# Batch 0 of an attention and mixing kernel: one group of scores weighted by a product on VectorE, fewer zero matmuls, one key tile for two query tiles

## The chip, the cores and the metric

The kernel runs on one core of a Trainium2 chip. The metric is the device time of one execution in microseconds (us); less is better. The core has five engines that the text names as the profile does: PE (TensorE, matmuls and transposes; PEld is its weight load), DVE (VectorE), ACT (ScalarE), POOL (GpSimd) and SP (SyncE, which here only starts transfers). Each engine works through its own instructions in order, and waits on semaphores for the others. Matmuls write to PSUM, from where VectorE or ScalarE fetch the result.

## The reference

The inputs are q, k, v of shape (4 batches, 8 heads, 768 tokens, 64) and the weights of a mixing layer; the output is (4, 768, 512) in float32. Cut to what matters:

```
rel  = pos[:, None] - pos[None, :]                  # 768 x 768
keep = (pos[None, :] < 8) | ((rel >= 0) & (rel < 96))
dist = where(global and not local, 96, |rel|)
scores = q @ k.T / 8 - slopes[h] * dist ; masked to -1e9 where not keep
a   = softmax(scores) ; x = (a @ v), heads side by side      # (B, 768, 512)
theta = x @ w_theta
y   = w_tok_r @ (x * cos(theta)) + w_tok_i @ (x * sin(theta))
u   = x + y
out = u + max(u @ w_ch, 0)
```

A query sees the 95 tokens before it, itself, and the first 8 tokens. With tiles of 128 tokens, a query tile therefore needs two key tiles: its own, and the one before it, whose first 8 rows can give way to the 8 global tokens.

## The kernel before, in words

**Tiles and groups.** There are six token tiles (NT). Heads are taken in pairs, `h0` = 0, 2, 4, 6. Scores stand with the keys on the partitions. `GROUPS` (line 198) lists the blocks (query tile, 1 for the key tile before it or 0 for its own) of a head pair in three groups: group 0 has (0,0), (1,1), (1,0), groups 1 and 2 have four blocks each. A group of both heads fills one PSUM tile `ps_w` (`ps_wide`, two buffers), which ScalarE turns to exponentials.

**The distance term, in two ways.** In batches 1 to 3, `att_scores` writes the scores alone, ScalarE takes the exponential into `e`, and `att_mul` multiplies it on VectorE by `wmask`, the exponential of minus slope times distance (also zero where masked), giving `p`. In batch 0, `att_bias` (line 242) first writes the distances into PSUM by matmuls of a scaled identity (`ident_d`) with `dist`, the scores are added on top, and ScalarE's exponential (line 272) gives `p` at once, with no product. `make_wmask` (line 192) makes the weights of one head by one ScalarE instruction.

**Steps of a head pair.** `att_transpose` (line 208) turns q and k of the pair on PE into two `ps_tr` PSUM buffers (of two) and copies them out, kT on ScalarE and qT on VectorE in batch 0. `att_extras` (line 231) makes the keys "before, with global rows" out of kT, on POOL (for pair 0 on VectorE); the groups 1 and 2 read them. `prepare_v` does the same for v. `att_values` (line 294) multiplies the probabilities with v into `ps_mm` buffers, `att_norm` (line 327) divides by the sums on VectorE, giving `x_sb`. `turn_x` (line 338) transposes a block of x on PE (into `ps_tr`) and copies it to `xT`; the variant "both" splits the copy between VectorE and ScalarE.

**Mixing.** `mix_theta` (line 356) multiplies xT with w_theta into `ps_w`, in pieces by dc (0 to 3, the head pair), and ends with cosine and sine on ScalarE (lines 372 and 373); `mix_z` multiplies them with x on VectorE; `setup_wtok` transposes the token weights, `mix_tok` sums over tokens, `mix_ch` does the last layer. In batches 1 to 3 attention of the next batch is laid between the mixing of the one before (`attend_beside`).

**What sets the order.** `K` keeps the order of the program text on each engine, so the order is written out by hand. Batch 0 stands at lines 500 to 545: in a loop over `h0` = 2, 4, 6 come the scores of groups 0 and 1, the values and normalisation of the pair before, the transposes of the next pair, the scores of group 2 and `turn_x`. Loads go through POOL's queue (`load_heads`, `load_wtok`, `load_weight`), in the order of the text, between POOL's copies.

**Zero matmuls.** `keep_warm(n)` issues n matmuls of zeros into a `ps_mm` buffer, `keep_warm_tr(n)` into a `ps_tr` buffer. Eight stand at the start of the program and two ahead of the first scores (line 509).

Of the kernel before, what the change touches and what calls it, by code (L numbers as in the profile page):

```python
# [16 lines left out]
def kernel(  # L17
# [13 lines left out]
    nc = tc.nc  # L31
    B, H, S, D = q.shape
    T = 128
# [20 lines left out]
    K = tc.keep_in_program_order  # L54
# [200 lines left out]
    def att_scores(b, h0, g_):  # L255
        qT, kT = qTs[b, h0], kTs[b, h0]
        blocks = GROUPS[g_]
        n = len(blocks)
        bias = b == 0
        if bias and (h0, g_) not in biased:  # L260
            att_bias(h0, g_)
        ps = biased[h0, g_] if bias else ps_wide()
        for i_, (it, prev) in enumerate(blocks):
            kc = it * T if prev == 0 else (0 if it == 1 else S + (it - 2) * T)
            for hh in range(2):
                R = slice(D * hh, D * (hh + 1))
                K(nc.tensor.matmul(ps[:, hh, i_ * T:(i_ + 1) * T],  # L267
                                   lhsT=kT[R, kc:kc + T], rhs=qT[R, it * T:(it + 1) * T],
                                   start=not bias, stop=not bias or i_ == n - 1))
        if bias:  # L270
            p = abuf.tile([T, 2, 4 * T], BF, name="p", bufs=6)
            K(nc.scalar.activation(p[:, :, 0:n * T], ps[:, :, 0:n * T], AF.Exp, scale=scale))  # L272
            probs[b, h0, g_] = p
            return
        e = abuf.tile([T, 2, 4 * T], BF, name="e", bufs=3)
        K(nc.scalar.activation(e[:, :, 0:n * T], ps[:, :, 0:n * T], AF.Exp, scale=scale))  # L276
        exps[b, h0, g_] = e
        att_mul(b, h0, g_)
# [58 lines left out]
    def turn_x(b, dc, by_dma, eng=nc.vector.tensor_copy):  # L337
# [10 lines left out]
        if eng == "both":  # L348
            K(nc.vector.tensor_copy(out=xT[:, 0:2 * T], in_=pt[:, 0:2 * T]))  # L349
            K(nc.scalar.copy(out=xT[:, 2 * T:], in_=pt[:, 2 * T:]))  # L350
        else:
            K(eng(out=xT, in_=pt))
# [147 lines left out]
    for h in range(6):  # L500
        make_wmask(h)
# [3 lines left out]
    att_transpose(0, 0, extras=False, between=lambda: att_bias(0, 1), cuts=(43, T))  # L505
# [3 lines left out]
    keep_warm_tr(2)  # L509
# [7 lines left out]
    for h0 in (2, 4, 6):  # L517
        att_scores(0, h0, 0)
        att_scores(0, h0, 1)
# [3 lines left out]
        if h0 < 6:  # L523
# [5 lines left out]
            att_scores(0, h0, 2)  # L529
# [3 lines left out]
    att_scores(0, 6, 2)  # L533
    mix_theta(0, 0, 0, 2)
    turn_x(0, 2, False, nc.scalar.copy)
    for h in range(6, H):
        make_wmask(h)
# [5 lines left out]
    mix_theta(0, 2, 0, 3)  # L543
    mix_theta(0, 0, 2, 3)
    turn_x(0, 3, False, "both")
# [89 lines left out]
```

## Time and profile before

| | |
|---|---|
| median of 3 runs | 175.93 us (175.57 to 175.95) |
| profiled execution | 177.43 us |
| its span, first to last instruction | 175.7 us |
| busy: PE, DVE, ACT, POOL | 165.6, 111.7, 103.8, 60.6 us |
| batch 0, first values of pairs 0, 2, 4, 6 on PE at | 13.20, 17.67, 22.20, 24.95 us |
| first cosine of batch 0 on ACT at | 28.88 us |

The profile is of one execution; times in it are us from the first instruction. A row of the timeline is: start, duration, engine, line of the kernel, operation, tile written and tiles read, shape and count; where rows of one kind follow each other they are merged, and the duration is that of all. Matmuls are pipelined: the row of a matmul is longer than the time until the next one starts, so the distance from start to start is what one takes of PE. A row of the waits is: who waited, for whom, us in total, how many times, the longest. In the slices each digit is a fortieth of the span, in tenths busy. The list of DMA issues gives for each transfer the time from issue to landing.

### The profile page before, as it was taken

The page shows a single profiled execution, that of the slowest core. Times are in us where ns is not written, and L with a number is a line of the kernel's source. Part 1 is how long each engine was busy: PE and PEld are TensorE (multiplying, and loading weights), DVE is VectorE, ACT ScalarE, POOL GpSimd, SP SyncE. Part 2 cuts the span into 40 slices and gives each one's busy share as a digit, 9 for nine tenths or more (in the row PEclk, how much of TensorE's full clock was granted, in tenths as well). Part 3 has the DMA queues.
Part 4 walks back from the last instruction along what each step waited for, and adds up shares of the span by engine and source line. Part 5 has one row for each costly group of instructions (what it writes and reads, how often), then busy time and mean ns, then how long its engine had stood idle before and what let it go on. Part 6 is the DMA issues. An engine that isn't in the chain of part 4 may idle for free.

```text
span 175.7 us, 4158 instructions
## 1 busy us (share of the span) xinstructions
PE 165.6 (94%) x1740; PEld 88.1 (50%) x1740; DVE 111.7 (64%) x205; ACT 103.8 (59%) x121; POOL 60.6 (35%) x99
## 2 busy tenths in 40 slices
PE   7889999899999999999998979999999999999992
PEld 2346665566465554445454544546555544444441
DVE  7756654975768784857567691857568784734353
ACT  5697889947777553797846712797756807500010
POOL 8986695004571400049716100049118000000000
PEclk9999999999999999999999999999999999999999
DMA  5999999999999944117999996116999433312325
GB/s 150 185 174 191 212 207 209 191 189 177 131 142 161 193 84 149 63 60 92 174 98 180 153 147 208 63 60 90 174 93 160 104 97 118 119 30 60 90 109 189
DMA packets 57058, 24.05 MB, mean 137 GB/s; under 512 B 43088, under 2 KB 54096, under 8 KB 57040
## 3 DMA queue, kind: packets, MB, share of 16 engines
q0 software_dynamic: 35328, 12.45, 65.8%
q1 hardware_dynamic: 21440, 10.95, 32.0%
q10 hardware_dynamic: 272, 0.39, 0.6%
q8 instruction: 13, 0.21, 0.5%
q14 instruction: 5, 0.04, 0.1%
HBM read 25.69 MB, written 6.29 MB: 182 GB/s over the span
## 4 chain that ended last, share of the span: by engine, by line
PE 56%; DMA 20%; ACT 9%; DVE 7%; POOL 4%; issue 2%; ACTq 0%
PE ps_mm L399 21%; PE ps_mm L441 10%; PE ps_w L364 9%; DMA v_sb<-in_v_dram 7%; DMA uTd<-u 6%; PE ps_tr L215 4%; PE ps_w L267 4%; DMA k_sb<-in_k_dram 4%; PE ps_w L315 3%; ACT kT L225 3%; DMA first<-in_q_dram 3%; ACT cs L373 2%; DVE w_tokT L117 2%; PE ps_w L252 2%; PE ps_mm L315 2%
## 5 line engine op out<-in xcount | busy, mean ns | idle before, releaser
L399 PE MATMUL ps_mm<-zri,w_tokT 128*128 128x512 bf16 x288 | 69.8, 380 | 0.1
L276 ACT ACTIVATE e<-ps_w 128x1024 bf16<-128x1024 f32 (+1 forms) x36 | 33.0, 951 | 19.6 <-PE ps_w L267 19.6
L399 PEld LDWEIGHTS <-w_tokT 128*128 128x128 bf16 x288 | 25.7, 98 | 28.2 <-issue 0.6
L233 POOL COPY kT<-kT 128x512 bf16<-128x512 bf16 x15 | 9.3, 622 | 64.6 <-ACT kT L225 64.6
L372 ACT ACTIVATE cs<-ps_w,halfpi 128x1024 bf16<-128x1024 f32 x12 | 13.4, 1115 | 19.7 <-PE ps_w L364 19.6
L441 PE MATMUL ps_mm<-w_ch_bf,uTd 128*128 128x512 bf16 x88 | 22.6, 380 | 1.4 <-DMA uTd<-u 1.4
L364 PE MATMUL ps_w<-w_theta_bf,xT 128*128 128x512 bf16 x96 | 22.9, 380 | 0.6 <-DVE xT L349 0.4
L404 DVE TENSOR_TENSOR u<-x_sb,ps_mm 128x512 bf16<-128x512 bf16 x24 | 16.2, 681 | 10.5 <-PE ps_mm L399 10.5
L288 DVE TENSOR_TENSOR p<-e,wmask 128x1024 bf16<-128x1024 bf16 x24 | 17.4, 725 | 8.5 <-ACT e L276 8.4
L380 DVE TENSOR_TENSOR zri<-cs,x_sb 128x1024 bf16<-128x1024 bf16 x24 | 16.1, 687 | 9.1 <-ACT cs L372 7.7
L444 DVE SCALAR_TENSOR_TENSOR o_sb<-ps_mm,u 128x512 f32<-128x512 f32 (+1 forms) x25 | 16.6, 664 | 2.8 <-PE ps_mm L441 2.7
L267 PEld LDWEIGHTS <-kT 64*128 64x128 bf16 x352 | 10.0, 94 | 14.7 <-issue 11.0
L267 PE MATMUL ps_w<-qT,kT 64*128 64x128 bf16 x352 | 16.2, 218 | 0.5 <-DVE kT L234 0.5
L225 ACT COPY kT<-ps_tr 128x768 bf16<-128x768 bf16 (+2 forms) x17 | 12.9, 765 | 4.9 <-PE ps_tr L215 4.9
L315 PEld LDWEIGHTS <-p 128*128 128x128 bf16 x352 | 12.9, 97 | 4.5 <-issue 0.8
L364 PEld LDWEIGHTS <-xT 128*128 128x128 bf16 x96 | 8.9, 98 | 11.3 <-DVE xT L349 0.6
L441 PEld LDWEIGHTS <-uTd 128*128 128x128 bf16 x88 | 8.0, 98 | 10.4 <-DMA uTd<-u 1.5
L80 POOL DMA_DIRECT2D v_sb<-in_v_dram x10 | 13.0, 1305 | 0.0
L286 DVE TENSOR_TENSOR p<-e,wmask 128x768 bf16<-128x768 bf16 x12 | 6.7, 559 | 9.9 <-ACT e L276 9.9
L272 ACT ACTIVATE p<-ps_w 128x1024 bf16<-128x1024 f32 (+1 forms) x12 | 11.3, 953 | 1.7 <-PE ps_w L267 1.2
L373 ACT ACTIVATE cs<-ps_w 128x1024 bf16<-128x1024 f32 x12 | 12.2, 1020 | 0.0
L91 POOL COPY v_pv<-v_sb 128x520 bf16<-128x520 bf16 x15 | 9.3, 620 | 8.3 <-DMA v_sb<-in_v_dram 8.3
(80 smaller groups left out, 192.4 us busy)
## 6 DMA issues: line engine op xcount, KB each, us to landing
out_dram<-o_sb SPq DMA_DIRECT2D x23, 256.0 KB, 2.2
q_sb<-in_q_dram POOLq DMA_DIRECT2D x6, 384.0 KB, 8.5
k_sb<-in_k_dram POOLq DMA_DIRECT2D x6, 384.0 KB, 10.1
v_sb<-in_v_dram POOLq DMA_DIRECT2D x6, 384.0 KB, 13.8
w_nat<-in_moe_w_tok_r_dram POOLq DMA_DIRECT2D x1, 1152.0 KB, 12.2
w_nat<-in_moe_w_tok_i_dram POOLq DMA_DIRECT2D x1, 1152.0 KB, 13.4
v_sb<-in_v_dram POOLq DMA_DIRECT2D x4, 192.0 KB, 7.3
q_sb<-in_q_dram POOLq DMA_DIRECT2D x3, 192.0 KB, 6.8
```

The costliest lines, as they stand in the source:

```text
L225: K(op(out=dst.rearrange("a (p t) -> a p t", t=NT)[:, p0:p1, :], in_=src.rearrange("a (t p) -> a p t", t=NT)[:, p0:p1, :]))
L267: K(nc.tensor.matmul(ps[:, hh, i_ * T:(i_ + 1) * T], lhsT=kT[R, kc:kc + T], rhs=qT[R, it * T:(it + 1) * T], start=not bias, stop=not bias ...
L276: K(nc.scalar.activation(e[:, :, 0:n * T], ps[:, :, 0:n * T], AF.Exp, scale=scale))
L288: K(nc.vector.tensor_mul(p.rearrange("a h (r x) -> a h r x", r=2), e.rearrange("a h (r x) -> a h r x", r=2), wmask[:, hs, None, T:3 * T].t ...
L315: K(nc.tensor.matmul(dst, lhsT=lhsT, rhs=rhs, start=(i_ == 0), stop=(i_ == len(mms) - 1)))
L364: K(nc.tensor.matmul(pth[:, s2, :], lhsT=xTs[b][:, dc, c:c + T], rhs=w_theta_bf[:, dc, :], start=(dc == 0), stop=(dc == NC - 1)))
L373: K(nc.scalar.activation(cs[:, :, 1, :], pth, AF.Sin))
L380: K(nc.vector.tensor_mul(zris[b][:, st:st + 2, wi, :].rearrange("a s (c d) -> a s c d", d=T), cs[:, :, wi, :].rearrange("a s (c d) -> a s ...
L399: K(nc.tensor.matmul(acc, lhsT=w_tokT[wi][:, st, tt * T:(tt + 1) * T], rhs=zris[b][:, st, wi, :], start=(done[b, tt] == 0), stop=(done[b, ...
L404: K(nc.vector.tensor_add(us[b][:, tt, :].rearrange("a (c d) -> a c d", d=T), x_sb[b][:, :, tt, :], acc.rearrange("a (c d) -> a c d", d=T)))
L441: K(nc.tensor.matmul(pc[:, 0:N], lhsT=uT[:, c:c + T], rhs=w_ch_bf[:, dc, cols], start=(dc == 0), stop=(dc == NC - 1)))
L444: K(nc.vector.scalar_tensor_tensor(o_sb, in0=pc[:, 0:N], scalar=0.0, in1=us[b][:, tt, cols], op0=ALU.max, op1=ALU.add))
```

## The change

In batch 0, group 1 of every head pair is made as in the later batches: no distance matmuls, the exponential into `e`, and a product with `wmask` on VectorE. In the loop this product stands after the normalisation of the pair before and the transposes of the next. All eight heads' `wmask` are made at the start. Ahead of the first scores, the bias matmuls of group 1 between the transposes of q and k give way to one zero matmul, and the two zero matmuls before the scores to one in a `ps_mm` buffer, which needs no `ps_tr` buffer. In all batches, the first key tile is used for the query tiles 0 and 1 in one matmul of 256 columns. `turn_x` of the last block copies both parts on VectorE, and the theta matmuls of dc 2 for the second pair of tiles stand after its transposes instead of before.

```diff
-    def att_scores(b, h0, g_):
+    def att_scores(b, h0, g_, mul=True):
         qT, kT = qTs[b, h0], kTs[b, h0]
         blocks = GROUPS[g_]
         n = len(blocks)
-        bias = b == 0
+        bias = b == 0 and g_ != 1
         if bias and (h0, g_) not in biased:
             att_bias(h0, g_)
         ps = biased[h0, g_] if bias else ps_wide()
-        for i_, (it, prev) in enumerate(blocks):
+
+        runs = [(0, 2)] + [(2, 1)] if g_ == 0 else [(i_, 1) for i_ in range(n)]
+        for i_, w in runs:
+            it, prev = blocks[i_]
             kc = it * T if prev == 0 else (0 if it == 1 else S + (it - 2) * T)
             for hh in range(2):
                 R = slice(D * hh, D * (hh + 1))
-                K(nc.tensor.matmul(ps[:, hh, i_ * T:(i_ + 1) * T],
-                                   lhsT=kT[R, kc:kc + T], rhs=qT[R, it * T:(it + 1) * T],
+                K(nc.tensor.matmul(ps[:, hh, i_ * T:(i_ + w) * T],
+                                   lhsT=kT[R, kc:kc + T], rhs=qT[R, it * T:(it + w) * T],
                                    start=not bias, stop=not bias or i_ == n - 1))
...
         exps[b, h0, g_] = e
-        att_mul(b, h0, g_)
+        if mul:
+            att_mul(b, h0, g_)
...
-        if eng == "both":
+        if eng == "halves":
             K(nc.vector.tensor_copy(out=xT[:, 0:2 * T], in_=pt[:, 0:2 * T]))
-            K(nc.scalar.copy(out=xT[:, 2 * T:], in_=pt[:, 2 * T:]))
+            K(nc.vector.tensor_copy(out=xT[:, 2 * T:], in_=pt[:, 2 * T:]))
...
-    for h in range(6):
+    for h in range(H):
         make_wmask(h)
...
-    att_transpose(0, 0, extras=False, between=lambda: att_bias(0, 1), cuts=(43, T))
+    att_transpose(0, 0, extras=False, between=lambda: keep_warm(1), cuts=(43, T))
     make_ident_d(2, 6)
     att_extras(0, 0, nc.vector)
     prepare_v(0, 0, nc.vector)
-    keep_warm_tr(2)
+    keep_warm(1)
     att_scores(0, 0, 0)
     att_scores(0, 0, 1)
...
     for h0 in (2, 4, 6):
         att_scores(0, h0, 0)
-        att_scores(0, h0, 1)
+        att_scores(0, h0, 1, mul=False)
         att_values(0, h0 - 2, apart=True)
         att_norm(0, h0 - 2)
         att_norm(0, h0 - 1)
...
                 load_heads(1, 0, 4)
-            att_scores(0, h0, 2)
+        att_mul(0, h0, 1)
+        att_scores(0, h0, 2)
+        if h0 < 6:
             turn_x(0, h0 // 2 - 1, False)
     load_heads(1, 4, 4)
     load_weight(w_ch_bf, moe_w_ch)
-    att_scores(0, 6, 2)
     mix_theta(0, 0, 0, 2)
     turn_x(0, 2, False, nc.scalar.copy)
-    for h in range(6, H):
-        make_wmask(h)
 
     K(nc.scalar.activation(halfpi_e, halfpi, AF.Sin))
     att_values(0, 6, apart=True)
     att_norm(0, 6)
     att_norm(0, 7)
-    mix_theta(0, 2, 0, 3)
+    mix_theta(0, 2, 0, 2)
     mix_theta(0, 0, 2, 3)
-    turn_x(0, 3, False, "both")
+    turn_x(0, 3, False, "halves")
+    mix_theta(0, 2, 2, 3)
     mix_theta(0, 0, 3, 4)
     mix_theta(0, 2, 3, 4)
```

## The prediction

> I write 4.1 for group 1 of the head pair that begins with head 4, and "exp 4.1" for its exponential on ScalarE. Times are us from the start of the span; times of the changed kernel are estimates, worked out from the rows named. An instruction that hands over on its own engine frees it some 0.05 before its recorded end, and a hand-over between engines takes about 0.05: both are read off neighbouring rows.
>
> **What bounds the kernel now.** First the page's busy shares and its slices (one digit is 4.39 us):
>
> ```profile
> span 175.7 us, 4158 instructions
> ...
> PE 165.6 (94%) x1740; PEld 88.1 (50%) x1740; DVE 111.7 (64%) x205; ACT 103.8 (59%) x121; POOL 60.6 (35%) x99
> ...
> PE   7889999899999999999998979999999999999992
> ...
> DMA  5999999999999944117999996116999433312325
> ```
>
> TensorE holds the kernel: no other engine is above 64%, and PE's only low digits lie in the first slices, once past the middle, and at the end. Whatever PE saves in batch 0 is therefore worth its time, if no one else becomes late. Second, PE's waits in the first 46 us, all of them:
>
> ```profile
> PE ps_mm L137 <- DVE zero L123: 1.2, 1, 1.2
> PE ps_w L267 <- DVE kT L234: 0.5, 1, 0.5
> PE ps_tr L215 <- DVE q_sb L503: 0.4, 1, 0.4
> PE ps_w L252 <- ACT p L272: 0.4, 1, 0.4
> PE ps_w L364 <- DVE xT L349: 0.4, 1, 0.4
> PE ps_tr L114 <- DVE w_tokT L117: 0.3, 1, 0.3
> PE ps_w L364 <- ACT cs L373: 0.2, 1, 0.2
> ```
>
> 3.4 us of 46, half of it before the first transposes; between 12.4 and 28 the list has none. Third, the timeline of PE in one turn of the batch-0 loop (pair 4):
>
> ```profile
> 15.77 0.49 PE L347 MATMUL ps_tr<-ident,x_sb 128*128 128x128 bf16 x6
> 16.11 0.49 PE L252 MATMUL ps_w<-dist,ident_d 128*128 128x384 bf16 x2
> 16.53 0.34 PE L267 MATMUL ps_w<-qT,kT 64*128 64x128 bf16 x6
> 16.82 0.59 PE L252 MATMUL ps_w<-dist,ident_d 128*128 128x512 bf16 x2
> 17.34 0.40 PE L267 MATMUL ps_w<-qT,kT 64*128 64x128 bf16 x8
> 17.67 0.27 PE L315 MATMUL ps_mm<-v_sb,p 128*128 128x65 bf16 x3
> ```
>
> From start to start: turn_x 0.34, bias of group 0 0.42, its scores 0.29, bias of group 1 0.52, its scores 0.33. One turn lasts 4.47 (values start at 13.20, 17.67, 22.20). The bias of group 1 is what the change takes out.
>
> **The parts that cost or give nothing by themselves.** *One key tile for two query tiles*: per group 0, six matmuls of 128 columns become two of 256 and two of 128. Rows of 6, 8 and 16 scores last 0.34, 0.40 and 0.62: 0.055 per pair of heads, and a 512-column matmul follows another after 0.216 (L364, four in 0.86), so 128 columns cost 0.054. The pair's time is the columns', and they stay. I take 0. The bound above is the whole 0.055 of the one pair dropped in each of the 12 groups after batch 0: 0.66 gained; nothing is added that could lose. *Eight weights first*: eight wmask rows 0.414 apart from 3.62 end at 7.04 instead of 6.2; ScalarE next works at 7.69, so the 1.49 idle before it hides them. Without that cover they cost 0.83. Two rows, 0.94, leave ScalarE at 25.84. *Scores 6.2 ahead of the last loads*: they stand in other queues than those loads (POOL's), so nothing.
>
> **The opening.** k's transposes started at 7.12, 0.53 after q's ended (6.59), behind two 512-column bias matmuls; one zero matmul is 0.216 plus about 0.1 for the change of shape, so they start near 6.90, and ScalarE's first kT piece 7.47 instead of 7.69. The other zero matmul, 0.3 with its change of shape, lies in the wait for that piece, from 7.2; the first scores follow the piece's end (7.85): 7.89 instead of 8.32, where two zeros stood in the way. Exp 0.0 follows the second kT piece, 8.28 (was 8.70). VectorE's kT extras still stand behind six ident_d rows (end 8.48), so scores 0.1 start 8.98 (was 9.17) and exp 0.1 ends 10.44 (was 10.63). Now the first new wait: VectorE's product for 0.1 (0.69, row L288) comes at 10.50 ahead of the copy qT of pair 2, which moves from 10.51 to 11.12 and ends at 12.06 instead of 11.45. Behind it wait scores 2.0, which start at 12.11 instead of 11.59. But bias 2.1, which sat until 12.30 waiting for exp 0.2 and then took 0.53, is gone: scores 2.1 follow at 12.28 (were 12.87), and the values of pair 0 start at 12.61 instead of 13.20. Exp 2.1 is even (13.25 against 13.30), bound by exp 2.0.
>
> **The loop.** I carry the same durations on. VectorE: the two normalisations take 1.40 up to qT (13.74 to 15.14), and follow the values: qT of pair 4 from 14.56 to 15.51. ScalarE: kT of pair 4 from 14.34 (end of the transposes; exp 2.1 ends 14.27), exp 2.2 15.16 to 16.18. PE: turn_x at 15.19 (was 15.77), bias and scores 4.0 until 16.23. Scores 4.1 need the PSUM buffer of exp 2.2 (16.23) and POOL's kT extras, which take 0.61 and 0.21 after kT (in the trace 15.78 to 16.67), so 15.20 to 16.08. Here is the second new wait. The product 2.1 stands in VectorE's queue behind qT, at 15.46, at the very time of POOL's copies. The trace shows what that costs, in two views of one place:
>
> ```profile
> 92.62 0.69 DVE L288 TENSOR_TENSOR p<-e,wmask 128x1024 bf16<-128x1024 bf16 x1 [0.35 <-ACT e L276]
> 93.53 1.10 DVE L288 TENSOR_TENSOR p<-e,wmask 128x1024 bf16<-128x1024 bf16 x1 [0.22 <-ACT e L276]
> ```
>
> ```profile
> 94.16 0.95 POOL L92 COPY v_pv<-v_sb 8x520 bf16<-8x520 bf16 x1
> 96.56 0.61 POOL L92 COPY v_pv<-v_sb 8x520 bf16<-8x520 bf16 x1
> ```
>
> A product beside POOL's copies takes 1.10 instead of 0.69, and a POOL copy 0.95 instead of 0.61: 0.41 and 0.34. The page GPSIMD Engine Reference of the Trainium skill (section "Key points") speaks against the change in the same sense: POOL shares its SBUF interfaces with VectorE and contends with instructions of two SBUF inputs. It gives no price, so by the rule alone there would be a loss of unknown size, down to none.
>
> I take the rows' price: POOL is done at 16.42, scores 4.1 start at 16.47 (16.23 without contention), values of pair 2 at 16.80 (were 17.67), with the product done at 16.56. What waits behind the product, the copy xT, ends at 17.06 before the transposes at 17.58 want its buffer. The next turn by the same steps: kT of pair 6 from 18.53, exp 4.2 19.35 to 20.37, POOL done at 20.62, scores 6.1 at 20.67, values of pair 4 at 21.00 (were 22.20). The turn falls from 4.47 to 4.20: PE gives 0.64 back, but 0.37 goes to waits for kT, exp and POOL.
>
> **The end of the loop.** Scores 6.2 end 22.61, exp 6.2 22.67 to 23.69 (was to 24.93); the product 6.1 stands behind the normalisations (22.97 to 23.66), beside POOL's DMA issues, where products kept 0.69 in the trace (80.98, during an issue of 80.31 to 81.76). The values of pair 6 start at 23.75 (were 24.95). xT of dc 2 ends on ScalarE at 24.77, the table load, 1.28, at 26.05: earlier than needed, since the two wmask rows no longer precede it. Six theta matmuls (1.29) then stand ahead of the last turn_x; it needs the normalisation, 25.76, and starts at 25.81; the two moved theta matmuls (0.43) fill the time of its copies, which removes PE's 0.4 wait for xT. The second half of xT on VectorE is 512 columns between the rows 0.29 (256) and 0.56 (768): 0.42, ends 27.0. The theta matmuls for dc 3 start at 26.68 (were 28.23), the first cs at 27.32 (was 28.88): 1.56 earlier.
>
> **What comes after.** From there ScalarE's cs rows (six in 6.0), VectorE's copies and PE's mixing follow each other as before. They need transfers that do not move: the weights of load_wtok(0), issued 13.45, land 12.2 later, 25.65, wanted at 27.6; those of load_wtok(1), 17.85 and 13.4, land 31.25, wanted at 32.4 (were 34.0); keys of batch 1, 23.10 and 12.2, land 35.3, wanted at 36.9. POOL issues them no later than now. w_theta, 10.09 and 10.0, lands 20.1, wanted at 22.5. None is late, so the 1.56 stays; I round to 1.6. Sum against the profiled execution: 177.43, of which 175.7 is span and 1.73 lies around it, gives 175.8. That execution is 1.5 above the median of the three, 175.93; a shift of the same size there gives 174.3.
>
> Bounds of the loop's costs: without the contention the two scores x.1 come 0.24 and 0.25 earlier, gain 2.05; with the contention also on the product beside DMA issues (as the ident_d rows at 3.5, 0.68 to 0.75 against 0.18) values of pair 6 slip 0.55, gain 1.0. So 173.9 to 174.9, and 173.3 with the 0.66 of the merged matmuls.
>
> **Rivals.** *Turn_x waits for qT's buffer.* It shares its PSUM slots with kT's and qT's transposes. Now it starts as kT's copy ends (15.72, start 15.77), before qT's does (16.09): it gets kT's slot. The zeros that also took one of these slots are gone, and the order in which slots come free may turn. Then turn_x starts 0.37 later in two turns: gain 0.9, 175.0. *A transfer takes the gain back.* Half the gain or all of it, if load_wtok(1) or the keys land 1.1 to 1.5 later than now or a transposing transfer of u (PE waits 1.4 for one at 105) meets other loads: 175.0 to 176.0, I write 175.6. For it: the DMA digits are 9 until 62. Against: POOL's queue only gets earlier.
> *Slower: TensorE's clock falls back.* The page's granted clock reads full throughout, but the zeros lie 0.43 apart until 4.6 (eight rows in 3.60) and 0.216 later; twelve transposes of q take 0.80 and those of k 0.53. So the array was at half speed until about 6.5, five us after its first work. The change takes 0.53 (bias) + 0.43 (two zeros) - 2 x 0.216 (the new ones), 0.53 us, of work from 6.6 to 9.0 and leaves a pause of 0.8 before scores 0.1, where the longest now is 0.5. If the array then runs at half speed for as long again, 5.3 us from 9.3, it loses 2.65, of which the 0.7 wait for qT absorbs a part: 1.9 more, 176.3. It decides from 4.6 us of half speed on. Against it, the pause is short beside the time it took to warm. The page "TensorE: Matmul & The Clock Gate" ("What's actually happening") asks for an idle window of about 3.4 us before half rate returns; by that rule this rival is out, and no row here tests it.
>
> **How the numbers follow.** The forecast of 174.3 (own range 173.8 to 174.9) gets 0.57; turn_x 0.14; a transfer 0.10, half of it within 0.2% (0.35 us, about what a measurement of this kernel can tell from no change); the clock 0.16; 0.03 for a loss that I don't see. Faster 0.57 + 0.14 + 0.05 = 0.76, same 0.05, slower 0.19. The range runs from the merged matmuls' bound, 173.3, to 176.0: it leaves out the clock, most of the 0.03 and little below.
>
> **What would show it.** Right: values of pairs 0, 2, 4, 6 near 12.6, 16.8, 21.0, 23.75; products of 1.1 in the turns of pairs 2 and 4; first cs near 27.3; later stages shifted whole. Wrong: turn_x starting after the end of qT; transposes of pair 2 at twice their 0.8 (clock); PE waiting for w_nat or k_sb after 28; scores of six columns' tiles not 0.34 but much shorter.

## The result, and the profile after

The changed kernel takes 174.37 us (median of 11 runs), the kernel before 176.18 us in the same series (11 runs). The ratio is 0.9877, with a 95% interval of 0.9848 to 0.9907: 2.2 us less, between 1.6 and 2.7. The forecast was 174.3 us, 1.6 us less than 175.93. The predicted time is met closely in part by luck: the kernel before came out 0.25 us higher in this series, and the gain is larger than the sum of the prediction's steps. (Ratios leave out executions that lie more than 1.5% above the fastest of the same kernel.)

The profiled execution took 173.99 us, 172.2 of it span. Its page, with the same lines as the page of before:

```profile
span 172.2 us, 4061 instructions
...
PE 160.9 (93%) x1677; PEld 86.7 (50%) x1700; DVE 114.9 (67%) x210; ACT 102.9 (60%) x120; POOL 61.0 (35%) x99
...
PE   7779999998999999999898999999999999999992
...
PEclk9999999999999999999999999999999999999999
DMA  4999999999999974117999995119995742222325
```

PE's busy time is 4.7 us lower and still 93%; VectorE gained 3.2 (five more instructions) and is still at 67%. Not all of the 4.7 was saved: 3.2 of it lie in three lines of the mixing that the change leaves alone, where this trace lacks 23 matmul records (276, 81 and 92 where the page of before has 288, 88 and 96, with as many weight loads as there). The granted clock reads full throughout. The span is 3.5 shorter, more than the ratio gives. Where the rest of that comes from shows in PE's waits between 80 and 120 us, the changed kernel's here:

```profile
PE ps_tr L215 <- DMA k_sb<-in_k_dram: 0.6, 1, 0.6
PE ps_w L319 <- POOL v_pv L92: 0.4, 1, 0.4
```

The same view of before has a wait of 1.4 us for `uTd<-u`, a transposing transfer of u:

```profile
PE ps_mm L441 <- DMA uTd<-u: 1.4, 1, 1.4
```

It is gone here, and no part of the change touches it. The first experiment asks whether it belongs to the kernel or to the one execution.

PE's waits in the first 46 us, against the list in the prediction:

```profile
PE ps_mm L137 <- DVE zero L123: 1.2, 1, 1.2
PE ps_w L270 <- DVE kT L234: 1.0, 1, 1.0
PE ps_w L270 <- DVE qT L225: 0.6, 1, 0.6
PE ps_mm L403 <- DVE w_tokT L117: 0.5, 1, 0.5
PE ps_w L270 <- POOL kT L234: 0.4, 2, 0.2
```

The two waits that the prediction announced are there: 0.6 for qT of pair 2 (0.7 was expected) and two of 0.2 for POOL. A third is longer than the prediction had it: the wait of scores 0.1 for VectorE's extras of kT grew from 0.5 to 1.0, where its rival on the clock names a pause of 0.8. One turn of the loop (pair 4), PE's timeline:

```profile
15.35 0.49 PE L351 MATMUL ps_tr<-ident,x_sb 128*128 128x128 bf16 x6
15.68 0.49 PE L252 MATMUL ps_w<-dist,ident_d 128*128 128x384 bf16 x2
16.10 0.34 PE L270 MATMUL ps_w<-qT,kT 64*128 64x256 bf16 x4
16.64 0.40 PE L270 MATMUL ps_w<-qT,kT 64*128 64x128 bf16 x8 [0.20 <-POOL kT L234]
16.97 0.27 PE L319 MATMUL ps_mm<-v_sb,p 128*128 128x65 bf16 x3
```

The two bias matmuls of group 1 are out, and a wait of 0.20 for POOL stands in their place. Scores of group 0 last 0.34 with four matmuls as they did with six.

Because executions differ by where their transfers fall, the table counts from the landing of the first part of q (5.0 to 5.2 us into the span), for three profiles of each kernel. The first pair is the first profile of each, the second comes from the first experiment, the third from the last, where one transfer of u is replaced in both kernels.

| us | before | changed | predicted for changed |
|---|---|---|---|
| first q to values of pair 0 | 7.98, 7.81, 7.99 | 7.68, 7.47, 7.76 | 7.40 |
| values of pair 0 to pair 4 (two turns) | 9.01, 9.00, 9.01 | 8.43, 8.42, 8.42 | 8.39 |
| values of pair 4 to pair 6 | 2.75, 2.75, 2.75 | 2.75, 2.75, 2.75 | 2.75 |
| values of pair 6 to the first cosine | 3.93, 3.93, 3.92 | 3.61, 3.61, 3.61 | 3.57 |
| sum: first q to the first cosine | 23.66, 23.49, 23.67 | 22.47, 22.26, 22.55 | 22.11 |
| first cosine of batch 0 to that of batch 1 | 39.89, 39.90, 39.90 | 39.71, 39.82, 39.71 | unchanged |
| batch 1 to batch 2 | 39.73, 37.52, 37.74 | 38.10, 38.25, 37.31 | unchanged |
| batch 2 to batch 3 | 36.88, 37.29, 36.97 | 36.57, 36.87, 36.76 | unchanged |

By the means, the first cosine is 1.18 earlier, where the prediction had 1.56: the opening gave 0.29 instead of 0.58, the rest of batch 0 gave 0.89 instead of 0.97.

### The profile page after: what moved, and what is told of

Its sections match the earlier page's. It is cut to its first block, busy times and chain, and to the rows that moved or that the text cites. A ratio compares the mean times of both kernels' runs of the same rounds, so it can differ in the third digit from the quotient of the medians.

```text
span 172.2 us, 4061 instructions
## 1 busy us (share of the span) xinstructions
PE 160.9 (93%) x1677; PEld 86.7 (50%) x1700; DVE 114.9 (67%) x210; ACT 102.9 (60%) x120; POOL 61.0 (35%) x99
## 4 chain that ended last, share of the span: by engine, by line
PE 68%; DMA 10%; DVE 8%; ACT 5%; POOL 4%; issue 3%; ACTq 0%
PE ps_mm L403 28%; PE ps_mm L445 11%; PE ps_w L368 10%; DMA v_sb<-in_v_dram 8%; PE ps_w L270 5%; PE ps_tr L215 5%; PE ps_w L319 4%; DMA first<-in_q_dram 3%; DVE w_tokT L117 2%; ACT e L279 2%; PE ps_mm L319 2%; DVE qT L225 2%; DVE zri L384 1%; PE ps_tr L114 1%; ACT kT L225 1%
## 5 line engine op out<-in xcount | busy, mean ns | idle before, releaser
L403 PE MATMUL ps_mm<-zri,w_tokT 128*128 128x512 bf16 x276 | 68.0, 380 | 1.4 <-DVE w_tokT L117 0.5
L279 ACT ACTIVATE e<-ps_w 128x1024 bf16<-128x1024 f32 (+1 forms) x40 | 37.1, 957 | 19.9 <-PE ps_w L270 19.8
L292 DVE TENSOR_TENSOR p<-e,wmask 128x1024 bf16<-128x1024 bf16 x28 | 20.0, 716 | 8.7 <-ACT e L279 8.7
L408 DVE TENSOR_TENSOR u<-x_sb,ps_mm 128x512 bf16<-128x512 bf16 x24 | 16.2, 682 | 10.5 <-PE ps_mm L403 10.5
L445 PE MATMUL ps_mm<-w_ch_bf,uTd 128*128 128x512 bf16 x81 | 21.5, 379 | 0.7 <-issue 0.5
L270 PE MATMUL ps_w<-qT,kT 64*128 64x128 bf16 (+1 forms) x320 | 16.0, 224 | 2.2 <-DVE kT L234 1.0
L270 PEld LDWEIGHTS <-kT 64*128 64x128 bf16 x320 | 9.2, 94 | 15.5 <-issue 11.6
L327 DVE TENSOR_TENSOR x_sb<-ps_w,rec 128x768 bf16<-128x768 f32 x12 | 11.5, 958 | 0.4
```

The lines of the kernel that those rows point to most:

```text
L270: K(nc.tensor.matmul(ps[:, hh, i_ * T:(i_ + w) * T], lhsT=kT[R, kc:kc + T], rhs=qT[R, it * T:(it + w) * T], start=not bias, stop=not bias ...
L292: K(nc.vector.tensor_mul(p.rearrange("a h (r x) -> a h r x", r=2), e.rearrange("a h (r x) -> a h r x", r=2), wmask[:, hs, None, T:3 * T].t ...
L403: K(nc.tensor.matmul(acc, lhsT=w_tokT[wi][:, st, tt * T:(tt + 1) * T], rhs=zris[b][:, st, wi, :], start=(done[b, tt] == 0), stop=(done[b, ...
L408: K(nc.vector.tensor_add(us[b][:, tt, :].rearrange("a (c d) -> a c d", d=T), x_sb[b][:, :, tt, :], acc.rearrange("a (c d) -> a c d", d=T)))
L445: K(nc.tensor.matmul(pc[:, 0:N], lhsT=uT[:, c:c + T], rhs=w_ch_bf[:, dc, cols], start=(dc == 0), stop=(dc == NC - 1)))
```

## The experiments

The theory is the prediction's: the gain is made in batch 0, by the bias matmuls that are gone from the loop (0.6), by the end of the loop (0.35), and by the opening (0.6); the merged scores are worth nothing, and POOL's contention with the new products costs 0.24 per turn. The rivals are that a transfer makes a part of the gain, that the merged matmuls do, and that the clock takes something back.

### Both kernels profiled again

No edit.

> The kernel before, profiled a second time. The changed kernel's profile was 1.3 us earlier at the first cosine of batch 0 and 3.4 us earlier at the end; 1.6 of the difference arose at 105 us, where the kernel before waited 1.4 us for the transposing transfer of u. Theory: that wait is not fixed by the program but by how the loads and transposing transfers fall in one execution; then a second profile of the same kernel has the first cosine at 28.9 again (within 0.2), but a wait at that place of another size, anywhere from 0 to 1.5. Rival: the wait belongs to the kernel; then it is 1.4 again, within 0.2.

> The changed kernel, profiled a second time. Both theories: the first cosine at 27.5, within 0.2. Theory of the single execution: waits for transfers between 80 and 120 differ from those of the first profile (0.6 for keys, none for u). Rival, the wait for u belongs to the kernel before alone: no wait for u here either.

The kernel before took 175.34 us (10 runs), 0.9992 of its own time in the comparison (0.9954 to 1.0031); the changed kernel 173.24 (6 runs), 0.9878 (0.9839 to 0.9917), the same as in the first series. In the new profile of before, PE does not wait for u at all between 100 and 110 us: the transfer took 8.4 us from issue to landing, not the 10.8 of the first profile. In the new profile of the changed kernel it took 10.5 (8.3 in the first), and PE waits for it. (The first fence is of PE and of its weight load: PE's row names a copy of VectorE that ended at the same moment, 102.48, but the weight load ahead of the same matmuls waited for u, which landed at 102.48.) In two kernels of the next experiments PE waits for u too (second and third fence). Waits between 80 and 125 us:

```profile
PE ps_mm L445 <- DVE xT L356: 0.9, 1, 0.9
PEld L445 <- DMA uTd<-u: 1.1, 1, 1.1
```

```profile
PE ps_mm L445 <- DMA uTd<-u: 0.5, 1, 0.5
```

```profile
PE ps_mm L445 <- DMA uTd<-u: 2.0, 1, 2.0
```

The wait is 1.4 and 0 in the kernel before, 0 and about 1 in the changed one, and up to 2.0 in the other kernels that carry the change. It belongs to the execution, as shown by both kernels having it both ways. Of the 3.5 between the first two spans, 1.6 therefore lies in a stretch where two single profiles say little (39.73 against 38.10 in the table's line of batch 1 to 2; in the second pair it is 37.52 against 38.25). The stretches of batch 0 repeat within 0.01 us in the loop and within 0.3 in the opening, so they can be read from one profile; the later ones can't. That the opening differs by so much had not been expected: the first cosine came at 28.48 and 27.27, where 28.9 and 27.5, each within 0.2, had been.

### The merged scores undone

```diff
-        runs = [(0, 2)] + [(2, 1)] if g_ == 0 else [(i_, 1) for i_ in range(n)]
+        runs = [(i_, 1) for i_ in range(n)]
```

> The changed kernel with six matmuls of 128 columns again in every group 0. Theory, a pair of heads costs PE the stream of its columns: the first cosine and every later stage stand where they do in the changed kernel, within 0.1 apart from waits for transfers; a row of four scores lasts as long as a row of six, 0.34. Rival, each dropped pair saves its whole 0.055: 12 groups after batch 0 make 0.66 us between the first cosine and the end.

Time 174.32 us (10 runs), ratio 0.9928 (0.9892 to 0.9963). PE's timeline in the turn of pair 6, and POOL's there:

```profile
17.71 0.77 PE L215 MATMUL ps_tr<-ident,k_sb 128*64 128x128 bf16 x12
...
20.20 0.34 PE L270 MATMUL ps_w<-qT,kT 64*128 64x128 bf16 x6
20.86 0.40 PE L270 MATMUL ps_w<-qT,kT 64*128 64x128 bf16 x8 [0.33 <-POOL kT L234]
```

```profile
19.45 1.08 POOL L233 COPY kT<-kT 128x512 bf16<-128x512 bf16 x1 [1.26 <-ACT kT L225]
```

Six scores last 0.34, as the four merged ones do. From the first cosine of batch 0 to that of batch 1 it is 39.72, against 39.71 to 39.82 in the changed kernel; from batch 2 to 3 it is 36.64, against 36.57 to 36.87. So in the batches after 0 the merge is worth nothing, as predicted, and the rival's 0.66 is not there. But in batch 0 the second turn is 0.38 longer (values of pair 0 to pair 4 in 8.81). The transposes of k for that turn took 0.77 where they take 0.50 in the turn before and in the changed kernel, at a full clock: eleven of the twelve kept their pace, and the last started 0.27 after the eleventh. ScalarE's kT came later, and the product then met POOL's large copy, which took 1.08 instead of 0.61. What held that one transpose is not shown by this one profile, and whether the merge has to do with it stays open. The ratio does not decide: its interval overlaps that of the changed kernel.

### The product ahead of the copy qT

```diff
         att_norm(0, h0 - 1)
+        att_mul(0, h0, 1)
         if h0 < 6:
             att_transpose(...)
...
-        att_mul(0, h0, 1)
         att_scores(0, h0, 2)
```

> The changed kernel with the product of group 1 ahead of the transposes of the next pair, so ahead of the copy qT in VectorE's queue. Theory, the product's place beside POOL's copies costs time: the product is 0.69 and POOL's small copy 0.21 again (0.93 to 0.96 and 0.55 in the changed kernel), PE's two waits of 0.2 for POOL go, and though qT ends 0.6 later, scores 4.1 start 0.1 earlier; the first cosine comes 0.1 to 0.3 earlier, near 27.3. Rival, qT is what PE waits for: scores of group 0 start 0.2 later in each of two turns, and the first cosine comes 0.3 to 0.5 later, near 28.0.

This is the test of the contention. In the changed kernel, VectorE's product and POOL's two copies of the turn of pair 4 lie on each other:

```profile
15.58 0.93 DVE L292 TENSOR_TENSOR p<-e,wmask 128x1024 bf16<-128x1024 bf16 x1
```

```profile
15.36 0.61 POOL L233 COPY kT<-kT 128x512 bf16<-128x512 bf16 x1 [1.08 <-ACT kT L225]
16.03 0.56 POOL L234 COPY kT<-kT 128x32 bf16<-128x32 bf16 x1
```

With the product ahead of qT they miss each other; the product and POOL's copies:

```profile
14.32 0.68 DVE L292 TENSOR_TENSOR p<-e,wmask 128x1024 bf16<-128x1024 bf16 x1
```

```profile
14.96 0.61 POOL L233 COPY kT<-kT 128x512 bf16<-128x512 bf16 x1 [1.08 <-ACT kT L225]
15.63 0.21 POOL L234 COPY kT<-kT 128x32 bf16<-128x32 bf16 x1
```

The product falls from 0.93 to 0.68 and POOL's small copy from 0.56 to 0.21, and both of PE's waits of 0.2 for POOL are gone; scores 4.0 now wait 0.15 for qT in their place. The two turns take 8.09 instead of 8.42. 0.16 of the 0.33 is given back between pairs 4 and 6 (2.91), so the first cosine is 0.17 earlier after the values of pair 0 (14.62 against 14.79). The contention is shown. The page GPSIMD Engine Reference of the Trainium skill (section "Key points") names it, for instructions with two SBUF inputs; here it has a price, 0.25 on the product and 0.35 on the copy. The time is 173.5 us (4 runs), ratio 0.9887 (0.9833 to 0.994): 0.17 is not to be told from the changed kernel there. The profiled execution took 176.23 us: it is the one with the wait of 2.0 for u, and after that wait the granted clock fell. The windows show it (columns: window, us, then busy time and count of PE, PEld, DVE, ACT, POOL, then the granted clock, DMA share and GB/s):

```profile
102.00:103.00 1.00, 0.00 (x0) 0.00 (x0) 0.00 (x0) 0.00 (x0) 0.00 (x0) 1.00 0.21 64
103.00:104.00 1.00, 0.78 (x3) 0.45 (x5) 0.00 (x0) 0.00 (x0) 0.00 (x0) 0.70 1.18 357
104.00:106.00 2.00, 2.00 (x5) 0.68 (x5) 0.69 (x1) 0.00 (x0) 0.00 (x0) 0.50 0.31 119
```

### Bias matmuls back, products out of the loop

```diff
-        bias = b == 0 and g_ != 1
+        bias = b == 0
...
-        att_mul(0, h0, 1)
         att_scores(0, h0, 2)
```

> The changed kernel with the distance matmuls back in group 1 of batch 0, and so without the products there; all other parts of the change stay. Theory: the products' turn is what shortens the loop. From the first values of pair 0 to those of pair 4 it took 9.01 us before and 8.42 in the changed kernel; here 9.0 (within 0.15). From the values of pair 0 to the first cosine 15.68 before, 14.79 changed; here 15.3, since the reordered end of the loop keeps its 0.35. Rival, the end of the loop and the opening made the gain: 8.4 and 14.8 as in the changed kernel.

One run, 173.71 us beside 175.42 for the kernel before. The turn of pair 4 on PE:

```profile
16.13 0.34 PE L270 MATMUL ps_w<-qT,kT 64*128 64x256 bf16 x4
16.42 0.59 PE L252 MATMUL ps_w<-dist,ident_d 128*128 128x512 bf16 x2
16.95 0.40 PE L270 MATMUL ps_w<-qT,kT 64*128 64x128 bf16 x8
```

The bias of group 1 is back, with 0.53 from its start to that of the scores, and no wait. The two turns take 9.01, as in the kernel before to the hundredth, and values of pair 0 to the first cosine 15.37. So the products in place of the bias are worth 0.58 in the loop, and the zeros, the merge and the early weights nothing there. That its one time lies as far below the kernel before as the changed kernel's says nothing: times of one kernel differ by more than 0.58 through the later waits.

### The tail of batch 0 undone

```diff
-            K(nc.vector.tensor_copy(out=xT[:, 2 * T:], in_=pt[:, 2 * T:]))
+            K(nc.scalar.copy(out=xT[:, 2 * T:], in_=pt[:, 2 * T:]))
...
-    mix_theta(0, 2, 0, 2)
+    mix_theta(0, 2, 0, 3)
     mix_theta(0, 0, 2, 3)
     turn_x(0, 3, False, "halves")
-    mix_theta(0, 2, 2, 3)
     mix_theta(0, 0, 3, 4)
```

> The changed kernel with the last turn_x copied by VectorE and ScalarE again and the two theta matmuls of dc 2 before its transposes again. Theory: PE's 0.4 wait for xT comes back, and the first cosine stands 15.1 to 15.2 after the values of pair 0 (14.79 changed). Rival, what helped at the end was the table load that two wmask rows no longer hold up: 14.8 here too.

One run, 173.38 us. Values of pair 6 to the first cosine take 3.93, as in the kernel before, and PE's wait is back:

```profile
PE ps_w L368 <- DVE xT L353: 0.4, 1, 0.4
```

The early table load is in this kernel too, and it gains nothing by itself: the tail's 0.32 comes from the two theta matmuls that fill the wait for xT, with the second copy moved to VectorE. From the first cosine to that of batch 1 it is 39.95, and over all profiles it is 39.71 to 39.82 in the ten with the new tail, 39.89 to 39.95 in the four without it. So the tail carries 0.1 to 0.2 more behind the first cosine; which instruction makes it was not traced.

### No zeros ahead of the first scores, and no zeros at all

```diff
-    att_transpose(0, 0, extras=False, between=lambda: keep_warm(1), cuts=(43, T))
+    att_transpose(0, 0, extras=False, cuts=(43, T))
...
-    keep_warm(1)
     att_scores(0, 0, 0)
```

> The changed kernel without its two zero matmuls ahead of the first scores (the eight at the start stay). Theory: they lie in waits and the clock does not need them; the transposes of pair 2 (24 in 0.64 from first to last start) keep their pace, and the values of pair 0 start up to 0.2 earlier, not later, measured from the landing of the first q. Rival, the clock falls back when PE works less here: the transposes of pair 2 take twice as long and the values of pair 0 start 0.5 to 1.5 later.

The second kernel also drops the eight zeros at the start of the program.

> The changed kernel without any zero matmul, the eight at the start included. Theory: the array needs some five us of work before full speed (the zeros start at 1.2, full pace from 6.5), so here it stays at half speed until some five us after the first distance matmul, near 9.5 to 10: k's transposes take twice their 0.31 from first to last start, and the values of pair 0 start 0.2 to 0.8 later. Rival, the zeros do nothing for the clock: everything stands as without the two.

The first expectation failed, in the sense of the slower rival. Single runs: 173.61 and 174.47 us. Without the two zeros, the values of pair 0 come 8.15 after the first q, not 7.64 (mean of the changed kernel). PE's timeline:

```profile
9.10 0.53 PE L215 MATMUL ps_tr<-ident,q_sb 128*64 128x128 bf16 x12
9.46 0.76 PE L215 MATMUL ps_tr<-ident,k_sb 128*64 128x128 bf16 x12
10.15 1.04 PE L252 MATMUL ps_w<-dist,ident_d 128*128 128x512 bf16 x2
11.12 0.61 PE L270 MATMUL ps_w<-qT,kT 64*128 64x128 bf16 x8
```

In the changed kernel these are 0.53, 0.50, 0.60 and 0.40. The windows name the cause, in the clock column (columns as above):

```profile
8.00:9.00 1.00, 0.23 (x8) 0.23 (x8) 0.71 (x4) 0.57 (x1) 1.00 (x2) 1.00 2.37 152
9.00:10.00 1.00, 1.00 (x30) 0.88 (x24) 0.96 (x2) 0.79 (x1) 1.00 (x2) 0.77 1.51 168
10.00:11.00 1.00, 1.00 (x7) 0.13 (x2) 0.98 (x3) 0.98 (x2) 0.88 (x2) 0.50 1.32 198
11.00:12.00 1.00, 1.00 (x11) 0.47 (x10) 0.83 (x1) 0.29 (x2) 0.82 (x3) 0.50 2.03 168
12.00:13.00 1.00, 1.00 (x11) 0.44 (x11) 0.00 (x0) 0.84 (x2) 0.94 (x2) 0.52 2.01 178
13.00:14.00 1.00, 1.00 (x32) 0.84 (x28) 0.21 (x2) 1.00 (x2) 1.00 (x2) 1.00 1.32 201
```

By the trace's record of the clock it rose at 6.13, fell to half at 9.55 and was back at 12.96: two stretches of 3.41 us. (The rise is the record's first entry; the column reads full ahead of it too, where matmuls still run at half their pace.) PE was not idle in the first of them. The window over that stretch, of this kernel and then of the changed one over the 3.41 us after its own rise, which the clock survived:

```profile
6.13:9.55 3.42, 1.89 (x48) 1.27 (x46) 2.97 (x13) 2.78 (x7) 3.42 (x5) 1.00 2.11 162
```

```profile
6.38:9.79 3.41, 2.23 (x40) 1.19 (x38) 3.11 (x12) 2.45 (x6) 3.41 (x5) 1.00 2.11 158
```

PE was busy for 1.89 where the clock fell, and for 2.23 where it stayed. But it may not be the whole busy time that decides, for more than half of the 1.89 are transposes. The same stretch with the matmuls on `ps_w` alone, which are all but the transposes, and then a stretch at the end of another kernel (the last one below, product ahead), where 512-column matmuls follow each other and then nothing:

```profile
6.13:9.55 3.42, 0.73 (x12) 1.00 2.11 162
```

```profile
167.32:170.74 3.42, 1.84 (x11) 1.00 0.73 273
```

The second has a little less PE time than 1.89, and the clock stayed full behind it. In all fourteen profiles the clock fell only at whole multiples of 3.41 us from its rise. Without the transposes all the stretches that begin at full clock fall into two groups: those with up to 1.06 us of other matmuls were followed by a fall, those with 1.30 and more were not (0.73 here; 1.51 in the changed kernel). With the transposes counted they don't quite: 1.84 and 1.95 stayed, 1.89 fell. That is one pair, 0.05 us apart, and ends of matmuls are modelled. So that the transposes do not count is the simpler reading of the traces, found afterwards; no run tested it.

Without any zeros the clock was first full at 13.28 (9.5 to 10 had been expected), and the values of pair 0 come 9.05 after the first q, 1.4 later than in the changed kernel; 0.2 to 0.8 had been expected.

The kernel without the two zeros was run once more, with more runs.

> The changed kernel without its two zero matmuls once more, timed and profiled again. In its first profile the granted clock rose at 6.1, fell to half at 9.5 and came back at 13.0, 3.41 us apart each time, and the values of pair 0 started 0.5 later; PE's matmul rows had filled 1.89 of the 3.41 us before the fall (2.15 or more in every profile of a kernel with the zeros, where it stayed). Theory, the clock is judged over stretches of 3.41 us that lie differently in each execution: the moment of the rise differs again, the clock falls in this profile if the stretch after it holds less than about 2 us of matmul rows, and the median is 0.2 to 0.6 slower than the changed kernel's, near 174.0. Rival, the first profile was a chance: no fall, values of pair 0 not later than 7.7 after the first q, and a time within 0.2 of the changed kernel's or below.

The clock again rose (5.78), fell (9.20) and came back (12.61), after a stretch with 1.77 us busy; values of pair 0 came 8.41 after the first q. The time is 174.27 us (10 runs), ratio 0.9877 (0.9836 to 0.9918), no different from the changed kernel's; 0.2 to 0.6 slower had been expected. The runs' mean granted clock helps here. One fall of 3.41 us at half speed is 0.99 over a span of 172 (1 - 0.5 x 3.41/172), and eight of these ten runs read 0.99: seven of them 173.99 to 175.16 us, one 176.49. The other two, at 0.998 and 1.0, are the two fastest, 172.63 and 173.44. So a fall costs about 1.2 us here by two runs against seven, and without one this kernel is no slower than the changed one (174.37, beside much the same time of the kernel before, 176.18 there and 175.95 here).

The same figure can be read for all the other runs. Of 64 of the kernel before whose clock is known, and 12 more with its transfer of u replaced, none reads below 0.995. Of the changed kernel's 17, one does, 177.95 us; of seven with the transfer of u replaced (next experiment) two do, 174.46 and 174.47, where the other five have a median of 173.05; of 21 runs of the variants with moved products or unmerged scores, two do. So the fall was seen only with the change, in 5 of 45 runs, and it costs 1.4 us where no wait for u is mixed in (two runs against five). Where in those executions the clock fell is known only for the profiled one, at 103, behind the wait for u and not in the opening. That the shorter work ahead of the first scores makes the other falls is likely, since without the two zeros nine of eleven runs have one, but not shown.

### The transfer of u taken out of both kernels

To measure the change without that wait, u of one tile (batch 1, tile 3) is transposed on PE, as is done elsewhere, in the kernel before, in the changed kernel and in the one with the product ahead:

```diff
-            if b < B - 1 or tt < NT - 2:
+            if (b, tt) != (1, 3) and (b < B - 1 or tt < NT - 2):
                 turn_u(b, tt)
...
         attend_beside(b + 1, tok_units(b, b > 0), 3 if b else 0, b + 2 < B)
+        if b == 1:
+            mix_uT(b, 3, 1, "act")
```

> The kernel before, with one of its transposing transfers taken away: u of batch 1, token tile 3, whose landing PE waited for in some profiles (0 to 2.0 us, near 103), is transposed on PE (four transposes, 0.22) and copied by ScalarE (0.59, idle there). Theory, that wait falls by the luck of an execution: PE no longer waits for u there, the stretch between the first cosines of batches 1 and 2 takes 37.1 to 37.5 us (39.7, 37.5, 38.1, 38.3, 40.8 in profiles that hold waits), and the time falls by 0.3 to 1.0. Rival, the next transfer is as late: the stretch stays at 38 or more and the time within 0.3 of before.

> The changed kernel with the same transfer taken away. Theory, batch 0 alone makes the gain of the change: 1.2 at the first cosine, 1.3 to 1.4 at that of batch 1, and no more from there; so it is 1.4 (0.8%) faster than the kernel before with the same transfer taken away, within 0.4. Rival, the change also shortens a later stage: the difference of the two stays near 2.1 (1.2%) as without this edit.

> As the one before it, with the product of group 1 ahead of the transposes of the next pair. Theory: the product's move is worth 0.17 from the values of pair 0 to the first cosine (14.62 against 14.79, seen in one profile), so this is the fastest of the three, by 0.1 to 0.3 us against the one before it. Rival: with PE less busy in the opening or another stage late, no faster.

| | median, runs | ratio to the kernel before | batch 1 to 2 |
|---|---|---|---|
| before, with this edit | 175.12 (12) | 0.9988 (0.9964 to 1.0012) | 37.74 |
| changed, with this edit | 173.41 (7) | 0.9901 (0.9861 to 0.9941) | 37.31 |
| product ahead, with this edit | 172.80 (7) | 0.9850 (0.9816 to 0.9883) | 37.43 |

PE no longer waits for u in any of the three. The kernel before gained 0.2 by its ratio, with no change inside the interval, not the 0.3 to 1.0 expected: in most of its executions the wait cannot have been long. Its stretch of batch 1 to 2 is 37.74, just outside the 37.1 to 37.5 expected, with a wait of 0.4 for a copy of v by POOL in it. The change is worth 0.9901/0.9988 = 0.9913 here, 1.5 us (1.7 by the medians), near the 1.4 expected, and this is the best measure of it. But the two intervals together leave about 0.7 to 2.3 (an estimate), so the rival's 2.1 is not ruled out; without the two runs whose clock fell the medians are 2.1 apart. The table fits the smaller figure, its line of batch 1 to 2 left aside: 1.18 at the first cosine, 0.15 up to batch 1, 0.31 between batches 2 and 3 (means of three), 1.6 together; of the last, the profiles of the other kernels show that it varies as much by itself (36.57 to 37.67). The version with the product ahead has the lowest time of all, 172.80 us, below the kernel before by 1.2 to 1.8%; its interval overlaps the changed kernel's, so that it beats that one too (by 0.6 in the medians, where 0.1 to 0.3 had been expected) is likely, not shown.

## Why the prediction was right, and where it was not

**Right in direction and place, and in the total's size partly by luck.** The bound was PE in batch 0, and what PE saves there arrives at the end: the first cosine came 1.18 earlier and nothing later gave it back.

**The loop: right.** Two turns in 8.42 where the steps gave 8.39; undoing the product alone gave the old 9.01. That PE gives back work in a turn and spends a part of it on waits was the right picture, with both terms too large: 0.64 and 0.37 were put down, and PE's busy time of a turn fell by 0.48 (4.41 to 3.93, means of two turns) while its idle time grew by 0.19. The two errors cancel. The contention was a little mis-sized: the product took 0.93 and 0.96, not 1.10, and POOL's added time was 0.35 against 0.34, but on the small copy. The price to PE, two waits of 0.20 for 0.24, is right, and the kernel with the product ahead shows it by taking it away.

**The end of the loop: right**, 3.61 for 3.57, and the product of pair 6 kept 0.68 beside POOL's DMA issues, as taken. **Merge, eight weights, table load: right at nothing** (for the merge, the one longer turn above stays open). The eighth weight ends at 7.02, and ScalarE still idles 0.34 before PE's transposes let it start kT at 7.37.

**The opening: mis-sized, 0.29 for 0.58.** It has two parts. From scores 0.1 to the values of pair 0 it takes 3.60, in all three profiles of the changed kernel, against 4.03, 4.02 and 4.03 before: the bias of group 1 of pair 2 is gone, the product and qT stand in the way, and the steps had 3.63. The part that failed is "VectorE's kT extras still stand behind six ident_d rows (end 8.48), so scores 0.1 start 8.98". From the first q to scores 0.1 it takes 4.08, 3.88 and 4.16, against 3.96, 3.79 and 3.96 before. The prediction had 3.77. Nothing was gained there, though the work ahead became shorter. (By execution it can be: with the same opening the kernel with the merged scores undone has 3.80, and that with the product ahead 3.75 in one profile and 4.13 in the other.) The extras are two copies on VectorE, and POOL issues DMAs beside them. VectorE and then POOL, first profile of the changed kernel:

```profile
8.26 0.32 DVE L233 COPY kT<-kT 128x512 bf16<-128x512 bf16 x1
8.61 0.50 DVE L234 COPY kT<-kT 128x32 bf16<-128x32 bf16 x1
```

```profile
8.34 0.77 POOL L75 DMA_DIRECT2D k_sb<-in_k_dram  x1
9.05 1.08 POOL L80 DMA_DIRECT2D v_sb<-in_v_dram  x1
```

The small copy, VectorE, in the kernel before and in the kernel with the merged scores undone, POOL's issue of k starting at 8.36 and 8.34 there:

```profile
8.91 0.20 DVE L234 COPY kT<-kT 128x32 bf16<-128x32 bf16 x1
```

```profile
8.54 0.17 DVE L234 COPY kT<-kT 128x32 bf16<-128x32 bf16 x1
```

Begun at 8.54 the copy passes in 0.17; begun at 8.61, 8.77, 8.81 or 8.91 in four other profiles, beside the same issue, it ends at 9.11 or 9.12, with the end of the issue. In the first profile of the kernel before it happened to start just ahead of that end. In the second profile of the changed kernel (3.88) the large copy is the one that is held, by the issue of q before that of k: begun at 8.16, it takes 0.45. The prediction gave a moved instruction its old duration; but what is fixed here is the end, and it goes with the end of POOL's issue (the last section has the figures where that end moves).

**After batch 0: too simple.** "The 1.56 stays" was right in that no weights or keys came late. But a further 0.3 to 0.5 came behind the first cosine (the 0.15 and 0.31 above), which no step foresaw. The 0.15 goes with the new tail; the 0.31 no experiment settled. And the first series measured 2.2 where the cleaner pair has 1.5. That 0.7 is within the two intervals, and may go with how the transfers between 80 and 120 us fell; more can't be said. The opening's shortfall and this surplus cancel in the total, which is luck.

**The rivals.** Turn_x never waited for qT. A transfer takes or gives up to 2 us, but by execution, not by the change. The clock was argued away for the wrong reason. The prediction set "the pause is short beside the time it took to warm" against it. No long pause was needed: a stretch of 3.41 us with 1.9 us of work in short pieces, 0.73 of it other than transposes, came before the fall. The page "TensorE: Matmul & The Clock Gate" of the Trainium skill ("What's actually happening") gives windows of that length that run freely, and the traces agree: 3.41, beginning at other moments in each execution. It also says that half rate follows an idle window. There the measurement differs: PE's rows filled 52 to 55% of the two stretches in the opening, and that was too little (as was 0.73 to 0.74 us, 21 to 22%, if the transposes do not count). The changed kernel has enough work there in most executions, thanks to the two zeros that stayed: both are matmuls of 0.39, and without them nine of eleven runs show a fall. The rival's 1.9 us was near the size too: a fall costs about 1.2 to 1.4. Its chance of 0.16 is about what 5 runs in 45 make of it, but it is a share of the executions, not one outcome for the kernel.

## What to carry to other kernels

When an edit moves an instruction, look up what the other engines do at its new place: a copy or a product has its trace duration only beside its old neighbours. Here a moved copy mostly gained nothing, since its end went with another engine's work, and a product made another copy 0.35 longer. Before taking filler work off PE, count PE's busy time in every stretch of 3.4 us around it, once without the transposes, and not the longest pause, and read the mean granted clock of all runs rather than of the one profile. And measure a change of 1% by a stretch that repeats (from a landing to a milestone) beside the total, since one transfer's luck here was as large as the gain.

## What the hardware showed that had not been expected

- **The clock goes by stretches of 3.41 us counted from its rise, and transposes may not count.** It fell after stretches with up to 1.06 us of matmuls other than transposes and stayed after 1.30 and more, in all fourteen profiles. Over all PE rows the border is less clean: 1.77 and 1.89 fell, 1.84 and 1.95 stayed. The rise itself comes 4.1 to 7.1 us into the span where the eight zeros stand at the start, and differs between executions of the same kernel: 6.38 and 6.11 in two of the changed one, 6.48 and 4.09 in two of the kernel before.
- **A DMA issue of POOL holds some VectorE copies until a fixed point, and the product not.** Besides the small copy above, the large one shows it. Begun at 8.00 to 8.31 while POOL issues the DMA of q, it ends 0.11 or 0.12 after that issue, and so moves with it: at 8.50 or 8.51 where the issue ends at 8.39 or 8.40, at 8.61 where it ends at 8.49, at 8.68 where it ends at 8.56 or 8.57 (0.36 to 0.51 us; 0.29 undisturbed). But not every copy is held: begun at 8.44, 8.48 or 8.59, inside the issue of k, the large copy takes 0.29, and in the first profile of the changed kernel 0.32 from 8.26. The product of pair 6 kept 0.68 from 23.14, beside issues that run from 22.74 to 24.91. How the issue does it is not shown.
- **Who comes second pays.** With POOL's large copy already running, the product takes 0.93 and POOL's small copy 0.56; where the product was first, it keeps 0.68 and POOL's large copy takes 1.08.
- **Columns set the pace of the scores, not the number of matmuls:** the scores of group 0, 384 columns for each of two heads, last 0.34 in four matmuls or in six.
- **The transposing transfer of u of batch 1, tile 3, took 8.3 to 11.0 us beside the loads,** varying between executions, and those behind 152 us, where no loads run, mostly 2.4.
